# Fused attention and highway layer: query transposes, row sums and value casts moved to other places in a written-out order, two adds of x done by TensorE

## The chip, the cores and the metric

One core of one Trainium2 chip runs the whole kernel. The metric is the device time of one launch in microseconds; the median of several runs is used. TensorE is called PE, VectorE DVE, ScalarE ACT, GpSimd POOL, and the queue that issues the transfers SP.

## The reference, cut to what matters

```python
def _attn_ref(q, k, v):            # each 8 batches x 8 heads x 576 rows x 64
    q_s = np.exp(q - max) ; q_s = q_s / sum over the 64 columns      # softmax of each query row
    k_s = np.exp(k - max) ; k_s = k_s / sum over the 576 rows        # softmax of each key column
    kv = np.einsum('bhsd,bhse->bhde', k_s, v)
    return np.einsum('bhsd,bhde->bhse', q_s, kv)

def _moe_ref(x, w_h, w_t, b_t):    # x: 4608 tokens x 512, from the attention
    H = np.maximum(x @ w_h, 0.0)
    T = 1.0 / (1.0 + np.exp(-(x @ w_t + b_t)))
    return T * H + (1.0 - T) * x
```

So for every batch there is a softmax of the queries, an unnormalised softmax of the keys times the values (its sums come from a column of ones beside the values), a product of the two, and then a highway layer on the 576 resulting rows of 512 columns. Inputs and output are float32; inside, the kernel works in float16 with float32 sums.

## The kernel before, in words

The work of one batch b has these pieces, each a function in the code:

- `load` (line 88) brings q, k and v of the batch through SP's queue. Each has three buffers.
- `exp_half` (L183) makes the exponentials on ACT, two halves for q and two for k. `cast_v` (L195) casts the values to float16 on POOL, in two halves.
- `q_sums` (L234) sums the query rows on DVE, again in two halves, one for each half of the heads; `q_recip` (L252) inverts all sums of the batch at once, so it needs both halves. `q_scale_p` (L264) multiplies the queries by them on POOL, in two parts: row groups 0 to 3 (128x1024) and 4 to 8 (128x1280), each over all heads, so that both need `q_recip`.
- `q_trans` (L69 on PE, L282 on DVE) turns the queries around on PE in three blocks (eight, eight and two transposes), through the one PSUM bank of the pool `ps_1`, and DVE copies each block out as `qsT`. For batches 6 and 7 (`turned`) two transposing transfers, `q_turn` (L291, tile `qsD`), do this instead; they wait in SP's queue for the scaling.
- `kv_half` (tile `psk`) multiplies keys and values on PE, 36 small products for each half, `kv_norm` (L222 and L223, tile `kvn`) normalises on DVE, `x_pair` (tiles `px` and `px_l`) multiplies by the turned queries on PE, and ACT copies the result out as `xT` (L354); a small rest goes through DVE (L315).

The highway layer runs in units (c, ob): batch c and block ob of 128 output columns, four to a batch; units 8 and 9 hold the ninth row groups of all batches.

- `gate` (tile `pt`): four products on PE, then a tanh on ACT (L383). `carry` (tile `ph`): four products on PE, then `dd` on DVE (L401). `blend` (L409): `g` from the two, on DVE. `gate` and `carry` take their PSUM banks from a pool of four, `ps_ht`.
- The term x is added to g in one of two ways. `add_x` (L421) adds it in place, on POOL or for a few units on DVE. Where a block is not in `added(g)`, `out_tile` adds it on PE: `turn_block` multiplies the block of `xT` by the identity into the same PSUM bank ahead of the block of g.
- `out_tile` (tile `nat`) turns four blocks of g around on PE for a pair of batches g (pair 1 is batches 2 and 3, pair 2 is batches 4 and 5), through the one bank of `ps_nat`; ACT copies the bank out (L461), and every fourth tile a transfer writes 1 MB.

Nothing is planned by a tool: the order on every engine is the order in which the functions are called. Each call is put at a position with `at(p, ...)`, the positions are sorted, and the calls are made in that order. A unit takes two positions and a batch eight, called a slot here: `gate(c, ob)` stands at 8c+2ob, `carry(c, ob)` at one more, `blend` at two more. While the highway layer of batch c runs, the attention of batch c+1 and the softmax of batch c+2 are placed between. For batch b the base is p = 8(b-1), and the tables hold offsets from it: `e0, e1` of the two query exponentials, `s0, s1` of the two row sums, `sc` of the scaling, `tr` of the three blocks of `q_trans`, `kv` of `kv_half` (with `kv_norm`) and `x` of `x_pair`. Each engine executes its own part strictly in this order, so an instruction that waits holds up all that stands behind it on its engine.

Of the kernel before, what the change touches and what calls it, by code (L numbers as in the profile page):

```python
# [18 lines left out]
def kernel(  # L19
# [10 lines left out]
    nc = tc.nc  # L30
    B, H, S, D = q.shape
    P = 128
    PAD = 128
    N9 = S // 64
# [125 lines left out]
    def two_banks(name, dt=FP32):  # L160
        return ps_2.tile([P, 2, 2048 // (4 if dt is FP32 else 2)], dt, tag="q2", name=name)
# [202 lines left out]
    def views(c):  # L364
        if c >= B:
            h = slice(4 * (c - B), 4 * (c - B) + 4)
            return lambda k_: x9[:, k_, h], lambda k_: g9[:, k_, h]
        g, b2 = c // 2, c % 2
        if g not in gT:
            gT[g] = gp.tile([P, 4, NM, 2, 64], FP16, tag="g", name=f"g_{g}")  # L370
        return lambda k_: xT[g][:, k_, :, b2, :], lambda k_: gT[g][:, k_, :, b2, :]
# [39 lines left out]
        )  # L411


    added = lambda g: ((0, 1), (0, 1, 2), (0, 1, 2), (0, 1, 2, 3))[g]
    added9 = lambda g: (0, 1, 2, 3) if g < 2 else (0, 1)

    def add_x(c, ob):
        xv, gv = views(c)
        late = ob == (3 if c == B - 1 else 2) and c % 2 and c < B
        eng = nc.vector if late else nc.gpsimd  # L420
        eng.tensor_add(gv(ob), gv(ob), xv(ob))  # L421


# [78 lines left out]
    def at(p, *fs):  # L502
        events.setdefault(p, []).extend(fs)

    E = lambda f, *a: (lambda: f(*a))

    for c in range(1, B + 2):
        for ob in range(4):
            p = 8 * c + 2 * ob
# [6 lines left out]
    for g in range(B // 2):  # L516
        p = 16 * (g + 1)
# [6 lines left out]
    p = 8 * B + 8  # L524
# [8 lines left out]
    at(10, E(cast_v_head, 2, 1, nc.scalar), E(exp_half, 2, "k", 1))  # L533
    at(10.5, E(blend, 0, 3))
    at(12.5, E(add_x, 0, 0), E(add_x, 0, 1), E(add_x, 1, 0))
    at(14.5, E(add_x, 1, 1))
    for c in range(2, B + 2):
        for ob in added(c // 2) if c < B else added9(2 * (c - B)):
            at(8 * c + 2 * ob + (2.5 if c < B - 1 else 2.02), E(add_x, c, ob))
    at(11, E(cast_v_head, 2, 2, nc.gpsimd), E(cast_v_head, 2, 3, nc.scalar))  # L540
    at(11, E(q_scale_p, 2, 8, N9))
    for b in range(2, B):
        p = 8 * (b - 1)
        if b > 2:
            e0, e1, s0, s1, sc = {
                3: (-2.6, -1.6, -1.1, -0.1, 1),
                4: (-5.5, -4.5, -2.8, -1.5, -1.4),
                5: (-5, -4, -3.4, -2.7, -2.6),
                6: (-6, -5, -3.95, -3.1, -3),
                7: (-6, -5, -3.95, -3.1, -3),  # L550
            }.get(b, (-5, -4, -3.9, -2.9, -2.8))
            at(p + e0, E(exp_half, b, "q", 0))
            at(p + e1, E(exp_half, b, "q", 1))
            at(p + s0, E(q_sums, b, 0))
            at(p + s1, E(q_sums, b, 1), E(q_recip, b))
            at(p + sc, E(q_scale_p, b, 0, 4))
            at(p + sc + (0.6 if b > 5 else 0), E(q_scale_p, b, 4, N9))
            s = p + {3: 0, 4: 0}.get(b, -0.5)
            at(s, E(exp_half, b, "k", 0), E(cast_v, b, 0))
            at(s + 0.9, E(cast_v, b, 1))  # L560
            at(s + 1, E(exp_half, b, "k", 1))
        tr, kv, x = {
            2: ((5, 6, 7.1), (4, 6.2), (6.5, 7.2)),
            3: ((4, 4.9, 4.95), (4, 4), (5.9, 6.9)),
            4: ((3, 4, 4.9), (4.5, 4.5), (5.9, 6.9)),
        }.get(b, ((2, 3, 4), (4, 4), (5, 6)))
        if b in turned:
            at(p - 1.05, E(q_turn, b, 0, 4), E(q_turn, b, 4, N9))
        else:
            for i in range(3):  # L570
                home = (lambda: two_banks("pq_t", FP16)[:, 0]) if b < 4 and i == 2 else None
                at(p + tr[i], E(q_trans, b, i, home))
        at(p + kv[0], E(kv_half, b, 0))
        if b == 2:
            at(p + kv[0], E(kv_norm, b, 0, 1))
            at(p + kv[1], E(kv_half, b, 1), E(kv_norm, b, 1, 2))
        else:
            at(p + kv[1], E(kv_half, b, 1), E(kv_norm, b))
        homes = (nat_bank, single) if b == 2 else None
        at(p + x[0], E(x_pair, b, 0, "AA" if b == 2 else "A", b > 2, homes))  # L580
        at(p + x[1], E(x_pair, b, 1, "AV" if b == 2 else "A", b > 2, homes))
# [70 lines left out]
```

The softmax here doesn't subtract the row's maximum and nothing guards it: scores larger than these inputs give would overflow.

## Time and profile before

| what | value |
|---|---|
| median of 5 runs (lowest to highest) | 130.19 us (129.63 to 131.16) |
| the profiled execution, its own time | 129.96 us |
| its span, from first to last instruction | 128.2 us |
| mean granted TensorE clock | 0.99 |
| PE busy | 111.3 us, 87% of the span |
| DVE busy | 99.4 us, 78% |
| ACT busy | 92.5 us, 72% |
| POOL busy | 77.7 us, 61% |
| `add_x` on POOL, 128x512 | 21 of 1153 ns |
| `add_x` on DVE, 128x512 | 3 of 986 ns in the mean |
| first part of `q_scale_p` on POOL | 9 of 1901 ns |
| second part of `q_scale_p` on POOL | 5 of 2403 ns |
| half a `cast_v` on POOL | 12 of 1146 ns |
| half a `q_sums` on DVE | 12 of 1346 ns |
| half an `exp_half` on ACT | 32 of 1176 ns in the mean |

The durations are those of single instructions; successive ones overlap by a little, so that the steps from start to start are some 0.05 to 0.1 us shorter. Busy time is no bound by itself: none of the engines is busy all the time, and the slots have waits on each of them. The profile's execution lies 0.23 us below the median, and 1.8 us of its time lie outside the span.

### The profile page before, as it was taken

To read this page: it belongs to the slowest core of one execution; us is meant where nothing else is said; L and a number is where in the kernel's file an instruction comes from. 1 tells how busy PE (TensorE), PEld (TensorE's weight loads), DVE (VectorE), ACT (ScalarE), POOL (GpSimd) and SP (SyncE) were. 2 spreads that over 40 slices of the span, in tenths; PEclk is the share of its full clock that TensorE was granted. 3 is DMA by queue.
4 is the path that set the end of the run, shared out by engine and by line. 5 is a ranking of instruction groups with operands and counts; after the bars stand their busy time and mean duration, and the time that the engine had idled before them with its cause. 6 is when DMAs were issued, how large, how long until landed. Compare 5 with 4: busy or idle time off the path is not lost.

```text
span 128.2 us, 3346 instructions
## 1 busy us (share of the span) xinstructions
PE 111.3 (87%) x1359; PEld 60.8 (47%) x1359; DVE 99.4 (78%) x181; ACT 92.5 (72%) x130; POOL 77.7 (61%) x73
## 2 busy tenths in 40 slices
PE   4988999986786998999769999995989999999940
PEld 2335443452344356555525564453445445579820
DVE  1297467787999999898599989983998656689960
ACT  4562099977988599679929995997897574757540
POOL 2005507960299999559946992799399745534510
PEclk9999999999999999999999999999999999999995
DMA  4999999999999999999999799999216906134994
GB/s 120 380 404 389 398 402 411 412 412 408 407 413 406 402 413 414 402 409 423 361 411 411 282 260 416 401 268 368 102 23 131 353 10 286 46 164 199 394 391 166
DMA packets 20583, 41.24 MB, mean 322 GB/s; under 512 B 5460, under 2 KB 5976, under 8 KB 19544
## 3 DMA queue, kind: packets, MB, share of 16 engines
q1 hardware_dynamic: 20568, 41.03, 85.5%
q8 instruction: 10, 0.16, 0.5%
q14 instruction: 5, 0.04, 0.1%
HBM read 30.41 MB, written 9.44 MB: 311 GB/s over the span
## 4 chain that ended last, share of the span: by engine, by line
PE 34%; DVE 32%; POOL 13%; ACT 7%; issue 6%; DMA 4%; SPq 0%; DVEq 0%; POOLq 0%; ACTq 0%
PE ph L64 9%; PE pt L64 9%; POOL eq L264 8%; DVE r L234 7%; DVE g L409 5%; DVE dd L401 5%; POOL v L195 5%; PE nat L64 4%; DMA q<-in_q_dram 4%; PE pq L69 3%; PE psk L64 3%; ACT eq L183 3%; PE warm L64 3%; DVE qsT L282 2%; ACT xT L357 2%
## 5 line engine op out<-in xcount | busy, mean ns | idle before, releaser
L64 PE MATMUL pt<-xT,w16t 128*128 128x512 f16 x128 | 33.6, 379 | 2.9 <-DVE dd L401 2.1
L264 POOL TENSOR_TENSOR eq<-eq,r 128x1024 f16<-128x1024 f16 (+2 forms) x16 | 30.1, 1897 | 9.2 <-DVE r L252 8.9
L64 PE MATMUL ph<-xT,w16h 128*128 128x512 f16 x128 | 33.3, 380 | 0.3
L383 ACT ACTIVATE pt<-pt,bt 128x512 f32<-128x512 f32 (+1 forms) x40 | 24.8, 622 | 7.4 <-PE pt L64 7.4
L421 POOL TENSOR_TENSOR g<-g,xT 128x512 f16<-128x512 f16 x21 | 23.9, 1153 | 7.9 <-DVE g L409 7.9
L409 DVE SCALAR_TENSOR_TENSOR g<-pt,dd 128x512 f16<-128x512 f32 (+1 forms) x40 | 25.2, 633 | 2.9
L401 DVE SCALAR_TENSOR_TENSOR dd<-xT,ph 128x512 f16<-128x512 f16 x32 | 21.7, 678 | 5.0 <-PE ph L64 4.8
L64 PEld LDWEIGHTS <-w16t 128*128 128x128 f16 x160 | 14.7, 97 | 19.1 <-issue 6.6
L183 ACT ACTIVATE eq<-q 128x1152 f16<-128x1152 f32 x16 | 18.2, 1177 | 3.3 <-DMA q<-in_q_dram 3.3
L183 ACT ACTIVATE ek<-k 128x1152 f16<-128x1152 f32 x16 | 18.6, 1175 | 1.1 <-DMA k<-in_k_dram 1.1
L195 POOL CAST v<-v 128x1152 f16<-128x1152 f32 x12 | 13.5, 1146 | 9.6 <-DMA v<-in_v_dram 9.4
L234 DVE TENSOR_REDUCE r<-eq 128x18 f32<-128x1152 f16 x12 | 16.0, 1346 | 3.9 <-ACT eq L183 3.9
L64 PEld LDWEIGHTS <-w16h 128*128 128x128 f16 x160 | 13.6, 98 | 10.5 <-ACT w16h L116 1.4
L64 PE MATMUL nat<-ident,g 128*128 128x128 f16 x142 | 16.0, 219 | 0.7 <-DVE g L409 0.4
L64 PEld LDWEIGHTS <-g 128*128 128x128 f16 x144 | 12.5, 98 | 7.6 <-DVE g L409 1.1
L461 ACT COPY o<-nat 128x512 f32<-128x512 f32 x26 | 15.6, 602 | 0.0
L354 ACT CAST xT<-px 128x1024 f16<-128x1024 f32 x10 | 10.2, 1017 | 7.4 <-PE px L64 7.4
L64 PE MATMUL warm<-wide,ident 128*128 128x512 f16 x41 | 12.1, 441 | 1.8 <-DVE wide L153 1.8
L69 PE MATMUL pq<-ident,eq 128*128 128x128 f16 x104 | 8.4, 219 | 2.3 <-DVE qsT L282 1.1
L357 ACT CAST xT<-px 128x512 f16<-128x512 f32 x8 | 4.3, 590 | 8.5 <-PE px L64 8.5
L282 DVE COPY qsT<-pq 128x1024 f16<-128x1024 f16 (+1 forms) x16 | 9.3, 587 | 0.9 <-PE pq L69 0.5
L69 PEld LDWEIGHTS <-eq 128*128 128x128 f16 x108 | 6.9, 97 | 5.5 <-issue 2.0
(57 smaller groups left out, 107.5 us busy)
## 6 DMA issues: line engine op xcount, KB each, us to landing
out_dram<-o SPq DMA_DIRECT2D x8, 1024.0 KB, 4.4
q<-in_q_dram SPq DMA_DIRECT2D x7, 1152.0 KB, 13.0
k<-in_k_dram SPq DMA_DIRECT2D x7, 1152.0 KB, 13.2
v<-in_v_dram SPq DMA_DIRECT2D x5, 1152.0 KB, 13.8
v<-in_v_dram SPq DMA_DIRECT2D x6, 576.0 KB, 11.6
q<-in_q_dram SPq DMA_DIRECT2D x2, 576.0 KB, 4.1
k<-in_k_dram SPq DMA_DIRECT2D x2, 576.0 KB, 6.5
w32t<-in_moe_w_t_dram SPq DMA_DIRECT2D x1, 1024.0 KB, 10.5
```

Source lines behind the costliest of these rows:

```text
L64: mm = lambda o, l, r, st, sp: nc.tensor.matmul(o, l, r, start=st, stop=sp, skip_group_check=True)
L69: nc.tensor.matmul(o, i, ident, is_transpose=True, start=True, stop=True, skip_group_check=True,)
L183: nc.scalar.activation(dst[b][:, :, 2 * a : 2 * a + 2, :], in32[which][b][:, 2 * a : 2 * a + 2].rearrange("p c n d -> p n c d"), AF.Exp,)
L195: (eng or nc.gpsimd).tensor_copy(o, i)
L234: nc.vector.reduce_sum(qsum[b][:, :, h], eq[b][:, :, h, :], axis=AX.X)
L264: nc.gpsimd.tensor_mul(e, e, r.broadcast_to(list(e.shape)))
L282: nc.vector.tensor_copy(qsT[b][:, :, n0:n1, :], t[:, :, 0:w, :])
L383: nc.scalar.activation(ps, ps, AF.Tanh, bias=bt2[:, ob : ob + 1], scale=0.5)
L401: nc.vector.scalar_tensor_tensor(dd, xv(ob), -0.5, ps, op0=ALU.mult, op1=ALU.max)
L409: nc.vector.scalar_tensor_tensor(gv(ob), th, 1.0, dd, op0=ALU.add, op1=ALU.mult)
L421: eng.tensor_add(gv(ob), gv(ob), xv(ob))
L461: nc.scalar.copy(o, flat(t))
```

## The change

Six things are different. (1) Blocks ob = 2 of pairs 1 and 2 leave `added`: for batches 2 and 4 the add on POOL goes, for batches 3 and 5 the add on DVE goes, and each of the 16 `out_tile` calls of the two pairs does one more transpose-like product of `xT` on PE (five blocks become six). (2) For batches 6 and 7 the first query exponential stands 0.6 earlier and the second 0.2 earlier, the first row sum 1.55 earlier and the second with its reciprocal 0.85 earlier, right behind `kv_norm` of the batch before. (3) Their scaling starts 0.9 earlier, and its two parts have the add of block 1 of the running batch between them. (4) `cast_v` of batches 5 to 7 is no longer tied to the key exponentials: both halves stand together, behind the scaling. For batch 5 they are at +0.4 instead of -0.5 and +0.4, and no other call on POOL stands between. (5) The three blocks of `q_trans` of batch 5 move from +2, +3, +4 to +0.9, +2, +2.9. (6) Those of batch 4 move from +3, +4, +4.9 to +2.5, +3.9, +4.4.

```diff
-    added = lambda g: ((0, 1), (0, 1, 2), (0, 1, 2), (0, 1, 2, 3))[g]
+    added = lambda g: ((0, 1), (0, 1), (0, 1), (0, 1, 2, 3))[g]
...
     def add_x(c, ob):
         xv, gv = views(c)
-        late = ob == (3 if c == B - 1 else 2) and c % 2 and c < B
-        eng = nc.vector if late else nc.gpsimd
+        eng = nc.vector if (c, ob) == (B - 1, 3) else nc.gpsimd
         eng.tensor_add(gv(ob), gv(ob), xv(ob))
...
                 5: (-5, -4, -3.4, -2.7, -2.6),
-                6: (-6, -5, -3.95, -3.1, -3),
-                7: (-6, -5, -3.95, -3.1, -3),
-            }.get(b, (-5, -4, -3.9, -2.9, -2.8))
+            }.get(b, (-6.6, -5.2, -5.5, -3.95, -3.9))
             at(p + e0, E(exp_half, b, "q", 0))
             at(p + e1, E(exp_half, b, "q", 1))
             at(p + s0, E(q_sums, b, 0))
             at(p + s1, E(q_sums, b, 1), E(q_recip, b))
             at(p + sc, E(q_scale_p, b, 0, 4))
-            at(p + sc + (0.6 if b > 5 else 0), E(q_scale_p, b, 4, N9))
-            s = p + {3: 0, 4: 0}.get(b, -0.5)
-            at(s, E(exp_half, b, "k", 0), E(cast_v, b, 0))
-            at(s + 0.9, E(cast_v, b, 1))
+            at(p + sc + (0.5 if b > 5 else 0), E(q_scale_p, b, 4, N9))
+            s = p + (0 if b < 5 else -0.5)
+            at(s, E(exp_half, b, "k", 0))
             at(s + 1, E(exp_half, b, "k", 1))
+            s = p + {3: 0, 4: 0, 5: 0.4}.get(b, -0.9)
+            at(s, E(cast_v, b, 0))
+            at(s + (0.9 if b < 5 else 0), E(cast_v, b, 1))
         tr, kv, x = {
...
-            4: ((3, 4, 4.9), (4.5, 4.5), (5.9, 6.9)),
-        }.get(b, ((2, 3, 4), (4, 4), (5, 6)))
+            4: ((2.5, 3.9, 4.4), (4.5, 4.5), (5.9, 6.9)),
+        }.get(b, ((0.9, 2, 2.9), (4, 4), (5, 6)))
```

## The prediction

> **What bounds the kernel now.** I read the page's head first, for which engine could be the limit at all, and then the same in the stretches that the change touches. The cuts are the ends of the key-value products (`psk`) of batches 4, 5, 6 and 7.
>
> ```profile
> span 128.2 us, 3346 instructions
> ...
> PE 111.3 (87%) x1359; PEld 60.8 (47%) x1359; DVE 99.4 (78%) x181; ACT 92.5 (72%) x130; POOL 77.7 (61%) x73
> ```
>
> Busy time by stretch (columns: length; busy us of PE, PEld, DVE, ACT, POOL; clock; DMA share; GB/s):
>
> ```profile
> 63.90:77.10 13.20, 11.71 (x163) 6.61 (x164) 12.29 (x20) 10.91 (x15) 10.01 (x8) 1.00 0.95 344
> 77.10:88.90 11.80, 10.24 (x141) 5.42 (x140) 9.02 (x15) 10.46 (x15) 8.56 (x7) 1.00 1.12 357
> 88.90:99.70 10.80, 10.26 (x141) 5.27 (x140) 9.70 (x15) 8.56 (x13) 8.69 (x7) 1.00 0.43 115
> 99.70:128.16 28.46, 23.23 (x209) 15.39 (x206) 19.03 (x38) 15.20 (x29) 11.48 (x13) 0.95 0.55 224
> ```
>
> No engine fills a slot, and PE, DVE and ACT are close together: whatever is taken from one is soon limited by the next. So the chain of waits, read from 77 to 100 us, says more:
>
> ```profile
> 77.31 0.42 DVE kvn L223
> 77.73 2.53 DVE r L234 x2
> 80.28 0.39 DVE r L252
> ...
> 82.69 2.33 POOL eq L264
> 85.02 1.11 POOL g L421
> 86.13 0.88 POOL v L195
> ...
> 87.15 1.16 POOL v L195
> ...
> 88.36 0.52 PE psk L64 x36
> ```
>
> This is a ring. The row sums of the next batch stand on DVE behind `kv_norm` (`kvn`), that waits for `psk`, that waits for the casts on POOL (`v`), these stand behind the scaling (`eq`), and that waits for the row sums. One turn is 88.88 - 77.06 = 11.82 us for batch 6; for batch 7, without an add on POOL, 99.71 - 88.88 = 10.83. After 99.7 the chain is PE almost without a gap.
>
> The two DVE adds that go, with the scaling beside them, from the timeline:
>
> ```profile
> 68.48 4.37 POOL L264 TENSOR_TENSOR eq<-eq,r 128x1024 f16<-128x1024 f16 x2 [2.91 <-DVE r L252]
> 68.89 1.77 DVE L421 TENSOR_TENSOR g<-g,xT 128x512 f16<-128x512 f16 x1
> 92.64 4.37 POOL L264 TENSOR_TENSOR eq<-eq,r 128x1024 f16<-128x1024 f16 x2 [2.11 <-DVE r L252]
> 94.06 0.76 DVE L421 TENSOR_TENSOR g<-g,xT 128x512 f16<-128x512 f16 x1
> ```
>
> Both adds end 0.28 us after the first part of the scaling (at 70.38 and 94.54): the add sits until that part is done, and the scaling beside an add takes 4.37 instead of 4.19, 0.18 more.
>
> **Part A, to the `psk` of batch 5 (63.9 to 77.1).** Removed: the DVE add, 1.77. The POOL add of batch 2 ends at 56.37, before the scaling of batch 4 could start (56.98), so it is worth 0. The third `q_trans` block of batch 4 now runs ahead of its `psk`; that `psk` still waits for its second cast (63.35). Behind it `x_pair` waited 1.13 for that block's copy and can start 1.2 earlier. These look like 1 to 2 us. But the queries of batch 5 are scaled only from their reciprocal on: two half sums of 1.26 from 64.50, one `dd` between, 68.11 instead of 68.31, since only a copy of 0.20 leaves from ahead of it. The first part of the scaling then ends at 68.28 + 1.90 = 70.18. The new order puts the first `q_trans` block ahead of `carry(4, 0)`, so PE, early by 1.2, stands there until 70.2. From there, in PE's order: block 0.45 (eight transposes of 0.056), `carry` 0.86, `gate` 0.86, six transposes of `out_tile` 0.34, block 0.45; then the third block directly behind the second, with one bank: result 0.16, copy 0.69, two signals 0.06, so PE idles 0.91; block 0.11, `carry` 0.86, `gate` 0.86, `out_tile` 0.34. Sum 6.04, so `psk` starts at 76.25; before it was 76.22. I take **0**. If PE's two waits vanished, `psk` would wait for the casts, which end near 74.8 (scaling to 72.5, two of 1.12): a bound of **-1.4**. The other bound is **+0.8**: a half sum (1.26) now stands in front of the last query copy on DVE, and only that engine's idle 0.47 before `kv_norm` is sure to take some of it.
>
> The batch 5 casts have no other POOL instruction between old and new place: nothing changes.
>
> **Part B, to the `psk` of batch 6 (11.82).** One half sum leaves the ring: -1.26. The add of `(4, 1)` enters it between the two parts of the scaling (+1.11), that of `(4, 2)` leaves it (-1.11). POOL alone would give -1.26. ACT doesn't: the exponential of batch 7 now stands ahead of the tanh of `(5, 1)` and the copy behind that. From ACT's starts (`xT` 78.45, next steps 0.94, 0.59, 0.48, 0.90, 1.06, 0.57, 0.48, 1.06, now 1.06, 0.56) that copy runs 86.15 to 86.75 instead of 85.09 to 85.73. PE needs its bank for the `out_tile` just ahead of `psk`, and DVE's first half sum of batch 7 waits for the exponential until 85.72, with `dd` (0.78) and `blend` (0.61) behind it. So `kv_norm` starts at 85.72 + 1.26 + 0.78 + 0.61 = 88.4, not 88.89. I take **-0.5**; bounds -1.26 and 0.
>
> **Part C, to the `psk` of batch 7 (10.83).** One half sum leaves (-1.26), the add of `(5, 1)` enters (+1.11) and here none leaves, the scaling without a DVE add beside it saves 0.18. Sum **-0.3**; PE, which loses two waits of 0.42 for `dd` (behind the DVE sums) and gets four more transposes, is there earlier. The turned queries keep their order in SP's queue: SP waits for the scaling, issues both transfers, and the output transfers stay behind them. If PE, there at 98.71 before, stays the limit, 0; if the add fits into POOL's idle 2.11 before the scaling, -1.4.
>
> **Part D, the rest.** PE's chain, and the six remaining tiles of pair 2 have a block more. In the chain a tile of six took 0.34 (58.82) and one of five 0.28 (104.81): 0.055 each, so **+0.3**. The ten other additional blocks lie in A to C, beside its waits. Bounds: 0 if PE's waits for `xT` near 104.2 cover them, and 6 x 0.22 = +1.3 if each cost the full duration of its matmul row (219 ns).
>
> A rule speaks for a higher price here. The Trainium skill, "TensorE: Matmul & The Clock Gate", section "Back-to-back issue gap", gives about 81 ns for a sustained pair of weight load and 128-column matmul. The trace shows 55 for the same pair; an estimate by that page is 6 x 81 = 0.5 us in this part and a total 0.2 later. The row decides.
>
> **Sum:** 0 - 0.5 - 0.3 + 0.3 = -0.5. The profiled execution took 129.96 (span 128.2 and 1.8 around it), so 129.5; the median lies 0.23 above it: **129.7**. About 1%, 1.3 us, is what a measurement of this kernel can tell from no change, so this is a forecast of no change.
>
> **Rivals.** (1) *Part A pays.* PE's waits of 1.1 and 0.9 there are made by order alone; if the blocks meet finished scaling, the freed DVE time counts: A -1.2 and the rest as above, -1.7, **128.5**. For it: the add was on the chain with its full 1.77. Against it: the scaling of batch 5 hardly moves. Chance 0.30.
> (2) *DVE waits for ACT at the early sums.* Place: the first half sums of batches 6 and 7, now in front of `dd` and `blend`. ACT has 10.4 us of starts in a slot of 11. If the exponentials come later than I place them by a copy, a tanh and an exponential (0.48 + 0.57 + 1.06 = 2.1), DVE stands 2.1 us twice, and PE runs out of banks behind it. Spare is 0.47 before `kv_norm` of batch 5, and 0.5 of part B's gain goes too: -0.5 + 0.5 + 2 x 2.1 - 0.47 - 1.94 (DVE's idle before `kv_norm` of batch 6) = +1.8, **132.0**. It decides from an exponential of batch 6 ending after 74.0, where DVE reaches the sum; I place its end near 73.2. Chance 0.16.
> (3) *The transposing transfers come late.* The add between the parts sends the second transfer of batch 7 off at 96.1. Before, such a one landed 3.4 us after its start, and `x_pair` needs it 3.6 after. If it takes 4.9, as the first of batch 6 did beside loads, it lands at 101.0 instead of PE's old 100.6: +0.4, with part D +0.7, **130.9**, still within 1%. Against it: no loads run by then. Chance 0.08.
>
> **How the numbers follow.** The forecast itself has 0.46, so within 1% is 0.46 + 0.08 = 0.54, faster 0.30, slower 0.16. The range reaches past rival 1 almost to the bounds of A and B together (130.19 - 1.4 - 1.26 + 0.3 = 127.8), to 128.0, and up to between rivals 3 and 2, 131.3, which leaves out most of rival 2 and little of rival 1.
>
> **What would show it.** Right: the scaling of batch 6 starts near 79.6 instead of 80.83 and that of batch 7 near 90.8 instead of 92.64; PE waits about 1.1 and 0.9 at the `q_trans` blocks of batch 5, where `psk` starts within 0.3 of 76.2; `psk` of batch 6 ends about 0.5 to 0.9 and that of batch 7 about 0.8 earlier; no add on DVE beside the scaling; tiles of pairs 1 and 2 of 0.34. Wrong: a `psk` of batch 5 a microsecond earlier (rival 1), row sums that wait over 2 us for exponentials with a longer slot of batch 6 (rival 2), `x_pair` of batch 7 waiting for `qsD` (rival 3), or additional blocks that cost 0.2 us each.

## The result and the profile after

The changed kernel took **131.94 us** in the median (130.9 to 133.61), the kernel before, run beside it, 130.9. The ratio is 1.008, with an interval of 1.0064 to 1.0097: 0.8% slower, about 1.05 us. That is within 1%, but it is a loss where a gain of 0.5 us was forecast, and it lies outside the range of 128.0 to 131.3. Some executions of any of these kernels are slower as a whole; the ratios compare the others alone, so that they can differ a little from the quotient of the medians, which are taken over all runs.

The profiled execution took 132.4 us. Head and queue table of the page of the changed kernel:

```profile
span 130.5 us, 3374 instructions
...
PE 111.9 (86%) x1375; PEld 61.1 (47%) x1375; DVE 97.6 (75%) x179; ACT 92.5 (71%) x130; POOL 75.5 (58%) x71
...
q8 instruction: 11, 0.18, 0.5%
```

DVE and POOL lost two adds each, and PE has 16 products and 16 weight loads more, as the diff says. The last line is the one that matters in the end: before, it read `q8 instruction: 10, 0.16, 0.5%`.

The two profiles can't be laid over each other from zero. The first loads land at different times from run to run (q of batch 1 at 17.62 us before, at 19.51 here), and at the first cast of batch 3, ahead of everything that the change touches, this execution is already 1.2 us late. I therefore measure from the start of `kv_norm` (`kvn`) of batch 3, 50.92 before and 52.26 here. The steps between the `kvn` starts of successive batches, in us:

| step | before | after |
|---|---|---|
| batch 3 to 4 | 13.24 | 13.24 |
| batch 4 to 5 (part A) | 13.15 | 13.34 |
| batch 5 to 6 (part B) | 11.80 | 11.30 |
| batch 6 to 7 (part C) | 10.88 | 10.56 |
| batch 7 to the end of ACT's last copy (part D) | 24.51 | 24.73 |
| sum, called the body below | 73.58 | 73.17 |
| last copy to the landing of the last output, called the tail | 2.62 | 3.99 |

The body became 0.41 shorter. The tail became 1.37 longer. Their sum, +0.96, is the loss. These are one profile of each kernel; the medians differ by 1.05.

The same stretches of the changed kernel, cut at `kvn` (columns as in the prediction: length; busy us of PE, PEld, DVE, ACT, POOL; clock; DMA share; GB/s):

```profile
65.50:78.84 13.34, 11.60 (x164) 6.55 (x162) 11.77 (x19) 11.50 (x15) 8.90 (x7) 1.00 1.02 371
78.84:90.14 11.30, 10.68 (x147) 5.58 (x145) 9.12 (x14) 10.16 (x14) 8.60 (x6) 1.00 1.05 319
90.14:100.70 10.56, 10.18 (x144) 5.47 (x143) 7.86 (x13) 8.75 (x13) 8.29 (x6) 1.00 0.46 126
```

The chain of waits of the changed kernel over these slots:

```profile
69.62 1.91 POOL eq L264
71.58 0.62 PE pq L69 x8
...
74.26 0.46 PE pq L69 x8
74.74 0.70 DVE qsT L282
75.49 0.27 PE pq L69 x2
...
77.82 0.73 PE psk L64 x72
...
86.06 1.20 ACT eq L183
87.28 1.35 DVE r L234
88.63 0.60 DVE dd L401
...
90.14 0.42 DVE kvn L223
90.57 1.27 DVE r L234
...
94.27 1.15 POOL g L420
95.42 2.17 POOL eq L264
97.59 0.06 issue
97.65 2.25 POOL v L195 x2
99.94 0.48 PE psk L64 x36
```

In the slot of batch 5 the chain goes from the scaling through the three `q_trans` blocks, that is, through PE's order. In the slot of batch 6 one half sum (`r`) is left behind ACT's exponential. In that of batch 7 the add `g` stands between the parts of the scaling. All three are as the parts A to C had them.

And this is the end of the run: DMA traffic from 122 to 131 us in 40 slices, and the transfers issued there (KB each, us from issue to landing). Kernel before:

```profile
GB/s 583 546 291 328 583 328 255 337 419 391 419 400 355 16 348 375 389 416 332 353 146 0 0 0 0 0 0 0 0 0 36 0 0 0 0 0 0 0 0 0
...
out_dram<-o SPq DMA_DIRECT2D x1, 512.0 KB, 3.3
out_dram<-o SPq DMA_DIRECT2D x1, 384.0 KB, 2.4
out_dram<-o SPq DMA_DIRECT2D x1, 128.0 KB, 2.4
```

Changed kernel, the same view:

```profile
GB/s 583 510 255 400 583 473 218 473 510 218 437 273 364 400 410 464 364 28 287 371 405 378 244 82 346 201 57 27 27 18 20 5 0 0 0 0 0 0 0 0
...
q8 instruction: 1, 0.02, 0.6%
...
out_dram<-o SPq DMA_DIRECT2D x1, 512.0 KB, 5.2
out_dram<-o SPq DMA_DIRECT2D x1, 384.0 KB, 4.0
out_dram<-o SPq DMA_DIRECT2D x1, 128.0 KB, 3.8
```

Before, the traffic stops from full rate, at once. After, it thins out at 18 to 27 GB/s for over a microsecond: about a sixteenth of the 400 GB/s before it, that is, one of the sixteen transfer engines working alone. And there is one packet of queue q8 among these outputs, of 16 KB, at 125.51. The three last outputs need 1.9, 1.6 and 1.4 us more to land. The sizes of the packets also point to one engine left behind: the 512 KB output moves in packets of 2 KB, and at 127.25 one of these is all that is under way, while the other engines have already moved their parts of the 384 KB output behind it.

SP's last issue is longer as well. Its rows, before and after (start, length):

```profile
124.73 0.41 SPq L497 DMA_DIRECT2D out_dram<-o  x1
...
125.66 1.14 SPq L496 DMA_DIRECT2D out_dram<-o  x1
```

The packet ends at 126.40 and the issue at 126.80. In the two other kernels below whose eleventh packet falls here, the issue takes 0.69 and 1.20 and ends 0.40 and 0.41 after the packet. One more thing falls into the longer tail: queue q14 brings an 8 KB code packet 1.9 to 2.7 us after the last copy in every kernel of this case; before, it came at 126.70, behind the last packet of the outputs, and here, at 128.01, it runs beside the delayed ones. How much it adds is not separated.

Queue q8 brings engine code, in packets of 16 KB. In both kernels ten of them lie between 17 and 111 us, each 0.9 to 1.4 us long, and they go with the count of PE's instructions (2481 of PE's 2730 recorded instructions, that is 2718 products and weight loads and 12 of its sequencer, had started at the tenth before, an average of 244 from one packet to the next, with single steps from 116 to 377). The changed kernel has 2762 on PE, and its eleventh packet came when 2759 had started. So the theory behind the experiments was: **the 32 additional PE instructions call for an eleventh piece of code, and it lands among the last outputs.** The rival was that the body lost the time, by one of the rivals of the prediction.

### The profile page after: what moved, and what is told of

Read it like the earlier page. It is cut to its first block, busy times and chain, and to the rows that moved or that the text cites. A ratio compares the mean times of both kernels' runs of the same rounds, so it can differ in the third digit from the quotient of the medians.

```text
span 130.5 us, 3374 instructions
## 1 busy us (share of the span) xinstructions
PE 111.9 (86%) x1375; PEld 61.1 (47%) x1375; DVE 97.6 (75%) x179; ACT 92.5 (71%) x130; POOL 75.5 (58%) x71
## 4 chain that ended last, share of the span: by engine, by line
PE 29%; DVE 20%; POOL 19%; DMA 11%; issue 7%; ACT 6%; SPq 3%; POOLq 0%; DVEq 0%; ACTq 0%
POOL eq L264 12%; DMA q<-in_q_dram 11%; PE ph L64 10%; PE pt L64 8%; DVE r L234 5%; DVE dd L401 5%; PE nat L64 4%; DVE g L409 4%; POOL g L420 4%; POOL v L195 3%; PE pq L69 3%; ACT eq L183 2%; PE psk L64 2%; SPq L96 2%; ACT w16h L116 1%
## 5 line engine op out<-in xcount | busy, mean ns | idle before, releaser
L420 POOL TENSOR_TENSOR g<-g,xT 128x512 f16<-128x512 f16 x19 | 21.7, 1154 | 5.7 <-DVE g L409 5.7
L64 PE MATMUL nat<-ident,g 128*128 128x128 f16 x142 | 16.9, 219 | 1.2 <-ACT o L460 0.6
L64 PEld LDWEIGHTS <-g 128*128 128x128 f16 x144 | 13.2, 98 | 8.2 <-DVE g L409 1.1
```

The source lines that it names most:

```text
L64: mm = lambda o, l, r, st, sp: nc.tensor.matmul(o, l, r, start=st, stop=sp, skip_group_check=True)
```

## The experiments

Each ran beside the kernel before, on the same chip. "R" in the expectations is the theory just told, and "refill" its word for such a code packet. The body and the tail are those of the table above, from one profile each.

**The two halves of the change.** First the additions alone, without the new order:

```diff
-    added = lambda g: ((0, 1), (0, 1, 2), (0, 1, 2), (0, 1, 2, 3))[g]
+    added = lambda g: ((0, 1), (0, 1), (0, 1), (0, 1, 2, 3))[g]
...
-        late = ob == (3 if c == B - 1 else 2) and c % 2 and c < B
-        eng = nc.vector if late else nc.gpsimd
+        eng = nc.vector if (c, ob) == (B - 1, 3) else nc.gpsimd
```

> The kernel before with only the four adds of x taken off POOL and DVE and the third blocks of pairs 1 and 2 given to PE; every position stays as before. Theory R (refill): the 32 more PE instructions make an eleventh 16 KB refill of PE's code fall into the last output transfers, which holds them up by about 1.2 us. The freed DVE add (1.77) and POOL add shorten the slots by about 1.3 to 1.5, the tail has 0.3 more, so the sum is -0.3 to 0 us against before, and the profile shows the refill after 120 us. Theory M (moves): the moved softmax work costs the time and the adds only help, so this kernel is 1 to 1.5 us faster than before, and a refill at the end, if any, delays nothing.

Measured: 133.63 against 130.88, ratio 1.0125 (1.0044 to 1.0206, wide because only three runs stand behind it): slower, but by how much is unclear. The tail is 3.93 with the eleventh packet at 125.80, as the theory has it. The body should have gained and is 1.50 longer: a miss. Up to `kvn` of batch 6 this kernel is ahead (87.71 - 51.08 = 36.63 against 38.19 before); then it loses 2.85 in the slot of batch 7. The waits there, and the chain, of this kernel:

```profile
PE px_l L64 <- DMA qsD<-eq: 2.0, 1, 2.0
```

```profile
84.75 5.63 DMA qsD<-eq
...
90.42 0.22 PE px_l L64 x2
...
93.17 1.82 PE ph L64 x4
94.99 1.00 PE pt L64 x4
```

The second turned query part of batch 6 took 5.63 us to land, and PE stood for 2.0. Behind that the four products of a `carry` took 1.82 instead of 0.86. The windows of this kernel say why (the number after POOL's is the granted clock):

```profile
88.00:90.40 2.40, 0.40 (x2) 0.10 (x1) 2.40 (x3) 0.61 (x2) 1.12 (x2) 1.00 1.08 418
90.40:93.00 2.60, 2.58 (x26) 1.43 (x25) 1.87 (x4) 2.06 (x3) 1.76 (x1) 0.76 0.13 54
93.00:95.00 2.00, 2.00 (x13) 0.78 (x8) 0.42 (x1) 2.00 (x3) 2.00 (x2) 0.50 0.33 66
95.00:97.00 2.00, 2.00 (x14) 1.02 (x13) 1.38 (x2) 1.16 (x3) 2.00 (x3) 0.96 0.53 101
```

PE's idle time was paid twice: once as the wait of 2.0, and once in a clock of 0.76 and then 0.50 over the next 4.6 us, by an estimate from these shares 2.6 x 0.24 + 2.0 x 0.50 = 1.6 us of PE's time. This is rival 3 of the prediction, in a slot where I had not placed it, and dearer. A piece of PE's code was also under way then (88.29, 1.06 us); how much of the 5.63 is due to that is not separated here.

Then the new order alone, with the four adds put back (the four lines above reversed in the changed kernel):

> The changed kernel with the four adds put back where they were, so that only the positions are moved and PE has as many instructions as before. Theory R: no refill near the end, the tail as before; the moved positions alone are worth 0 to +0.6 us against before. Theory M: the moved positions cost what the change cost and the benefit of the adds is missing as well, so +1 to +2.5 us.

Measured: 131.37 against 130.88, 1.0032 (0.9991 to 1.0073). PE's count is that of before again, there are ten packets, and the tail is 2.52. The body is 0.52 longer. So the tail belongs to the products on PE, and the new order by itself wins nothing.

**Adding and taking PE instructions alone.** In the kernel before, 32 PE instructions more at the very beginning, where PE waits for the first loads (a product of two columns in place of some of the warm-up's wide ones):

```diff
+    def tiny(n):
+        for _ in range(n):
+            mm(warm[:, 0:2], ident, wide[:, 0:2], True, True)
...
-        E(warm_up, 24),
+        E(warm_up, 22), E(tiny, 18),
```

> The kernel before with 16 more PE products in the first warm-up (22 of 512 columns and 18 of 2 columns instead of 24 of 512), which ends before PE's first real work as it did: 32 more PE instructions, nothing else. Theory R: +0.8 to +1.4 us, with an eleventh refill of PE's code after 120 us and last output transfers that land later after the last ACT copy than before (2.6 us). Theory M: within 0.3 us of before.

Measured: 132.9 against 130.88, 1.013 (1.0081 to 1.0178). Nothing of the work was touched, and yet the last outputs look like those of the changed kernel. DMA view from 122 to 131 us:

```profile
q8 instruction: 1, 0.02, 0.6%
...
out_dram<-o SPq DMA_DIRECT2D x1, 512.0 KB, 5.2
out_dram<-o SPq DMA_DIRECT2D x1, 384.0 KB, 4.1
out_dram<-o SPq DMA_DIRECT2D x1, 128.0 KB, 3.9
```

The tail is 4.16. The body is 0.55 longer as well, all of it between `kvn` of batches 3 and 4 (13.79 instead of 13.24); I did not trace why.

The reverse: the changed kernel with 32 PE instructions fewer in its warm-up (fillings of a tile on DVE keep the start of the warm-up late, so that it ends where it did):

```diff
-    nc.vector.memset(wide, 0.0)
+    for _ in range(7):
+        nc.vector.memset(wide, 0.0)
...
-        E(warm_up, 24),
+        E(warm_up, 16),
...
-        E(warm_up, 6),
+        E(warm_up, 2),
...
-        E(warm_up, 4),
+        E(warm_up, 2),
...
-        ... E(warm_mid, 5),
+        ... E(warm_mid, 3),
```

> The changed kernel with 16 fewer warm-up products (the first 24 become 16 that start later, 6 become 2, 4 become 2, 5 become 3): 32 fewer PE instructions, as many as the kernel before. Theory R: no refill near the end, 0.8 to 1.4 us faster than the changed kernel, so -0.4 to +0.3 us against before; if the shorter warm-up slows the early products, up to 0.4 of it is lost. Theory M: as slow as the changed kernel, +1 us against before.

Measured: 130.25 against 130.88, 0.9952 (0.9925 to 0.9979): 0.6 us faster than before, where the changed kernel is 1.05 slower. Its page and its DMA view from 122 to 131 us:

```profile
span 128.1 us, 3348 instructions
...
q8 instruction: 10, 0.16, 0.5%
```

```profile
out_dram<-o SPq DMA_DIRECT2D x1, 512.0 KB, 3.3
out_dram<-o SPq DMA_DIRECT2D x1, 384.0 KB, 2.4
out_dram<-o SPq DMA_DIRECT2D x1, 128.0 KB, 2.3
```

Tail 2.53, body -0.42. With the refill gone, the body's gain is the kernel's gain.

The control: the same trim in the kernel before, which has no eleventh packet to lose.

> The kernel before with the same 16 fewer warm-up products as the trimmed changed kernel (32 fewer PE instructions than before). A control for the shorter warm-up. Theory R (a refill of PE's code delays what shares its transfer engine): before had no refill in its last outputs to lose, so -0.3 to +0.3 us. Rival W: the shorter warm-up itself is what made the trimmed changed kernel faster, and this kernel gains about 1.5 us as well.

Measured: 130.5 against 130.47, 0.9997 (0.9968 to 1.0027); body and tail 73.58 and 2.53. The trim by itself is worth nothing, so that what the trim won in the changed kernel is the refill's, not the warm-up's.

**Count or place?** If the eleventh packet only hurts because of where it falls, still more instructions should move it ahead of the outputs. The kernel before with 208 PE instructions more:

```diff
+            mm(warm[0:32, 0:2], ident[:, 0:32], wide[:, 0:2], True, True)
...
-        E(warm_up, 24),
+        E(warm_up, 12), E(tiny, 116),
```

> The kernel before with 104 more, very small PE products in the first warm-up (12 of 512 columns and 116 of 2 columns on 32 weight columns): 208 more PE instructions. Theory R: what counts is where a refill falls. The eleventh now falls near 113 to 115 us, into an output transfer that is not the last ones, so -0.2 to +0.7 us against before, clearly less than the +2.0 of the kernel with 32 more. Rival N: each additional PE instruction costs, and this kernel is at least as slow as that one, +2 us or more. A start that is late by up to 0.5, since the small products may outlast the wait for the first queries, is told from both by the first products' time.

Measured: 131.0 against 130.47, 1.0053 (1.0016 to 1.009), less than half of the 1.3% that 32 instructions cost. The eleventh packet came at 118.99, later than expected but still ahead of the last outputs, and it was all but alone there: from 118.95 to 119.9 the trace has two packets in all. The tail is 2.54, and the body 73.59, that of before. What is left lies ahead of `kvn` of batch 3, which starts at 52.56. The small products did not keep the clock up (0.50 granted from 9 to 12 us and 0.60 from 12 to 16, where the kernel before has 1.00; 0.966 in the mean of the run), and the first sixteen query transposes took 1.90 us, where before each eight took 0.6. How much of the late start is due to that is not separated from the loads, which land at different times in each run. For the tail, then, it is the place, and not the number of packets, that costs.

**What the change could have given.** The trim with the additions alone (the first experiment without its refill):

> Only the four adds are given to PE, positions as before, and 32 fewer PE instructions through the shorter warm-up. Theory R: no refill in the last outputs, and the refill that held the turned queries of batch 6 near 88 us comes some 1.5 us later; the shorter slots count: -0.8 to -1.6 us against before. Rival L: the turned queries of batch 6 land late in any case since they stand behind the loads of batch 7, PE stands still for 2 us and then runs at half clock as in the kernel with the adds alone: 0 to +1 us.

Measured: 129.3 against 130.47, 0.9903 (0.9867 to 0.9939). Body -1.27, tail 2.53. The wait that had spoiled the first experiment is short here:

```profile
PE px_l L64 <- DMA qsD<-eq: 0.6, 1, 0.6
```

And the trimmed changed kernel with the three blocks of `q_trans` of batch 5 back at their old places:

```diff
-        }.get(b, ((0.9, 2, 2.9), (4, 4), (5, 6)))
+        }.get(b, ((2, 3, 4), (4, 4), (5, 6)))
```

> The changed kernel with the shorter warm-up, and the query turns of batch 5 back at +2, +3, +4. Theory of the sum: the two PE waits at these turns (1.1 and 0.9 us, the changed kernel's trace shows them) take up what the removed DVE add gives in the slot of batch 5; without them psk of batch 5 comes 0.8 to 1.2 us earlier and the kernel is 0.5 to 1.0 us faster than the trimmed changed kernel (-1.1 to -1.7 us against before), unless the turned queries of batch 6 then land too late. Rival: the waits lie beside others, and this kernel is as fast as the trimmed changed kernel.

Measured: 129.19 against 130.47, 0.9913 (0.9881 to 0.9945); body -1.41. The step from `kvn` of batch 4 to 5 is 12.34 instead of 13.34 in the same kernel with the moved blocks. That full microsecond is what the early blocks cost. The waits of the changed kernel around it (65.3 to 78.6 us):

```profile
PE pq L69 <- POOL eq L264: 0.9, 1, 0.9
...
PE pq L69 <- DVE qsT L282: 0.8, 1, 0.8
```

In this version the first of the two is gone, and only a weight load waits 0.3 for the scaling, where in the changed kernel it waits 1.1; the second, for the one bank, is there with 0.8 as before.

Both versions were then given their loads 0.05 positions earlier, ahead of the output transfer that stands at the same place of SP's queue, to take away the last wait for `qsD`:

```diff
-        at(8 * (b - 3), *[E(load, b, w) for w in "qkv"])
+        at(8 * (b - 3) - 0.05, *[E(load, b, w) for w in "qkv"])
```

> The four adds on PE, old positions, shorter warm-up, and each batch's loads put 0.05 ahead of their old place, so that in SP's queue the loads of batches 6 and 7 come before the output transfer of the same position instead of behind it. PE waited 0.6 us there for the turned queries of batch 6. Theory D (the turned queries stand behind the loads, which stand behind a 1 MB output): they land 2 to 4 us earlier, PE's wait for them goes, -0.2 to -0.6 us against the kernel without the earlier loads, so -1.2 to -1.6 against before. Rival P: the slot ends with POOL's casts anyway, and the gain is under 0.2 us.

> The changed kernel with the query turns of batch 5 back in their old place, the shorter warm-up and the same earlier loads. PE did not wait for the turned queries in the kernel without the earlier loads, so both theories expect 0 to -0.3 us against it, -1.1 to -1.5 us against before; slower than that would mean that the delayed 1 MB output then comes into the way of later transfers.

Measured: 129.59 against 130.8, 0.9912 (0.9874 to 0.995), and 129.67 against 130.8, 0.9916 (0.9882 to 0.995). PE's wait for `qsD` is gone in the first of them, and yet neither gains: the bodies are -1.53 and -1.42, but the tails 3.16 each, 0.6 longer than without the step. Two things differ at the end. The last output is issued 0.65 us after ACT's last copy in the first of them, 0.23 without the step; why is not shown. And the 8 KB code packet of q14 starts at 125.53 and 125.51, among the last outputs, where without the step it started at 126.45 and 126.28, behind their last packet. That is the place of the eleventh packet again, with a smaller packet of another queue; here no run separates it from the later issue.

## Why the prediction failed, by its own steps

Of the 2.2 us between the forecast of 129.7 and the 131.94, 0.7 are not the change's: the forecast started from the 130.19 of five runs, and beside the changed kernel the kernel before took 130.9. The other 1.5 lie between a forecast of -0.5 and a measured +1.05.

**Part A, forecast 0, was +0.2** (13.15 to 13.34). The two waits that I put at 1.1 and 0.9 were 0.9 and 0.8, and `psk` started at 76.5 on the clock of the kernel before (77.82, less the 1.34 of the late start) where I had 76.25. Undoing the move of the blocks brought the step to 12.34: the freed add is worth 0.8, and the order of PE ate it, as the part argued. Rival 1 was right that there is a gain to be had in this part, 0.8 where it put 1.2, and wrong about the kernel as it is.

**Part B, forecast -0.5, was -0.5** (11.80 to 11.30). The limit is ACT, as placed: the first half sum of batch 7 waited 0.9 us for its exponential. The scaling of batch 6, on POOL's timeline of the changed kernel:

```profile
81.10 1.90 POOL L264 TENSOR_TENSOR eq<-eq,r 128x1024 f16<-128x1024 f16 x1 [3.99 <-ACT xT L354]
82.96 1.15 POOL L420 TENSOR_TENSOR g<-g,xT 128x512 f16<-128x512 f16 x1
84.07 2.33 POOL L264 TENSOR_TENSOR eq<-eq,r 128x1280 f16<-128x1280 f16 x1
...
92.41 1.90 POOL L264 TENSOR_TENSOR eq<-eq,r 128x1024 f16<-128x1024 f16 x1 [2.71 <-DVE r L252]
```

It starts at 79.76 on the old clock, against a forecast of 79.6; that of batch 7 at 91.07 against 90.8. The first row names a copy on ACT as what ended the wait; the reciprocal ended at 80.93, as close before the start (0.17) as that of batch 7 at 92.24, so I read both as waits for the reciprocal.

**Part C, forecast -0.3, was -0.3** (10.88 to 10.56). `psk` of batch 7 came 0.6 earlier in all, not 0.8: part A's +0.2.

**Part D, forecast +0.3, is the term that failed.** PE's share of it was sized well: 24.51 to 24.73 is +0.2, and tiles with six blocks took 0.34, so that the trace's 55 ns for a pair of weight load and product held, and the 81 ns that the Trainium skill gives ("TensorE: Matmul & The Clock Gate", section "Back-to-back issue gap") were not seen here. But the part costed the 16 additional products only at their time on PE, and the sum took everything behind the last instruction of the chain as it was. Measured, this term is 0.2 on PE and 1.4 on the last transfers: **+1.6 instead of +0.3.** With part A's +0.2, that turns -0.5 into +0.96 in the profile, where +1.05 was measured in the median.

There was a warning to be read, though not a forecast. The page of the kernel before had the line on q8; the trace has the times of its ten packets; and at an average of 244 recorded PE instructions to a packet, with 2481 at the tenth, the eleventh was due near 2725, five short of the 2730 that the kernel has. With single steps from 116 to 377, that is good to some hundred instructions at best. A kernel that stands so close to its next piece of code, and is given 32 instructions more, is a case for a rival of its own.

The Trainium skill describes the mechanism ("Runtime: NRT & Kernel Launch", section "Instruction fetch mechanics"): each engine's code comes in blocks of 16 KiB through the sequencer's own queue, and the cost of a block is called mostly hidden. The 16 KB agree with the packets here. For PE's own work the chains of waits shown here agree: none of them stops PE for a packet. For the transfers that are under way beside one, the section says nothing; here the cost shows, in a tail of 3.99 instead of 2.62.

**The rivals.** Rival 2 (DVE waiting 2.1 us for exponentials) did not come: the wait was 0.9, and part B had it. Rival 3 (turned queries late) did not come in the changed kernel, but did in the first experiment, for 2.0 us and with a halved clock behind it.

## What to carry to other kernels

Before costing an edit that adds instructions, look at the code packets in the queue table and at the count of instructions at each: an edit that brings one more packet pays where that packet falls. Here it paid 1.3 to 1.6 us in the tail among the last outputs, and nothing there ahead of them. A sum over the chain of engines ends with the last output's landing, not with the last instruction, so give the transfers behind it a line of their own. And when a change mixes several moves, run them apart: here the additions on PE alone, without the extra packet, shorten the body by 1.3 us, the early query blocks cost 1.0 of it, and 129.2 to 129.3 us, 0.9 to 1.0% below the kernel before, was to be had.

## What the runs showed of the hardware

A code packet of 16 KB takes 0.9 to 1.7 us, and outputs of 128 to 512 KB that are under way meanwhile landed 1.3 to 1.9 us later, in three kernels (the changed one, the additions alone, and the padded one before); the same packet at 118.99, ahead of the last outputs and with almost nothing else under way, cost nothing in the tail (2.54). In the same three kernels SP's last issue ended 0.40 us after the packet and took 0.69 to 1.20 us instead of 0.41.

A PE wait of 2.0 us for a transfer was followed by a granted clock of 0.76 over 90.4 to 93.0 and 0.50 over 93.0 to 95.0, so that four 512-column products took 1.82 instead of 0.86: with the estimated 1.6 us from above, the price of this one wait was nearly doubled.

With 116 products of two columns in place of 12 wide ones, the granted clock was 0.50 from 9 to 12 us, where the wide ones had kept it at 1.00 (0.966 in the mean over the run, against 0.99).

Open are the 0.55 us of the padded kernel between batches 3 and 4, the later last issue with the earlier loads, the share of the q14 packet in the longer tails, and the share of the code packet in the late `qsD` of the first experiment.
